# Top-k attention and a GELU block on one core: the search for the 32nd largest score split into sorted pairs, with the pairs' smaller halves made on GpSimd

## The chip, the cores and the metric

The kernel runs on one core of one Trainium2 chip. The metric is the device time of one execution in microseconds (us). Below, PE is the TensorE, DVE the VectorE, ACT the ScalarE, POOL the GpSimd and SP the SyncE, whose queue issues nearly all DMAs. All data is float32 in SBUF with 128 partitions; "128x576" means 128 partitions with 576 elements each.

## What is computed

For 8 batches of 8 heads with 576 tokens of 64 values each, the 32 largest scores of every row are kept, the rest is pushed to minus infinity, and the softmax of the row multiplies v. The result, put side by side by heads as 4608 tokens of 512 values, goes through two matrix products with an exact GELU between them.

```
scores = scale * np.matmul(q, k.transpose(0, 1, 3, 2))          # 576 x 576 per head
kth = np.partition(scores, -top_k, axis=-1)[..., -top_k:-top_k + 1]   # top_k = 32
scores = np.where(scores >= kth, scores, -1000000000.0)
scores = scores - np.max(scores, axis=-1, keepdims=True)
attn = np.exp(scores); attn = attn / (np.sum(attn, axis=-1, keepdims=True) + 1e-09)
attn_out = np.matmul(attn, v)
h = x @ w_in                                                     # 4608 x 512 by 512 x 2048
out = (0.5 * h * (1.0 + erf(h * inv_sqrt2))) @ w_out             # 2048 x 512
```

## The kernel before, in words

The attention works in 144 items. One item is 128 score rows of each of two heads, so two rows of 576 scores per partition (tile `s`, 128x1152, in five buffers). The main loop (L659) runs one step n per item and holds several items at once: in step n it forms the scores of item n+2 on PE and copies them to SBUF on ACT (L301, L302), searches item n on DVE (`top_k`, L329), does the softmax of item n-1 on ACT (L383 and L384), and transposes item n-2 on PE (L415, L433). Every second step multiplies a finished pair of items by v (L470) and copies the product to `xT` (L475). The rest of PE's time in a step goes to pieces of the two matrix products (L522 and L558), eight pieces a step as soon as enough tokens are in `xT`, which is from step 10 on. In the steps before that, `keep_busy` (L633) fills PE with multiplications whose result is thrown away. After the last item PE alone finishes the pieces that are left. The order on every engine is the order in which the code issues the instructions.

`top_k` finds the 32nd largest of 576 scores for both rows of an item: four rounds of MAX8 (the eight largest, L344), and after each of the first three a replacement of the eight found by a very small number (L347, which the profile shows as a short MATCH_VALUE_LOAD and a MATCH_REPLACE8). The hook in the last round is `inverse` (L370), DVE's reciprocal of the softmax sum of the item before; it waits for `add_small` (L376) on POOL, and that waits for the softmax on ACT.

POOL's order in a step is: the first addition of a weight block (`weights_add`, L198), `add_small` of item n-1 (L376), the second addition (`weights_end`, L210; it comes directly behind the first in the late units), `threshold` of item n (L359 and L362, which wait for the search), and `normalise` of item n-1 (L396, two multiplications of 128x576 by the reciprocal). PE's transposes of item n-1 in step n+1 wait for `normalise`.

The weights are brought in 16 units, loaded by SP from L160 as words shifted by two bytes and put together by ACT (L175, L177, L179) and POOL. Ten units are made in steps 1 to 10 (START is 10), six more in steps 13 to 18. In the six late units POOL also does ACT's third operation (L195), and `normalise` is done by DVE in five of those steps. Four of the units are staged in a tile of its own (`words`), the others in a part of `w_out_sb` that isn't used yet.

Of the kernel before, what the change touches and what calls it, by code (L numbers as in the profile page):

```python
# [8 lines left out]
TOPK = 32  # L9
LOWEST = -3.4028234e38  # L10
# [4 lines left out]
def kernel(  # L15
# [19 lines left out]
    nc = tc.nc  # L35
    f32, i32, u32 = mybir.dt.float32, mybir.dt.int32, mybir.dt.uint32
    bf16, i16, u16 = mybir.dt.bfloat16, mybir.dt.int16, mybir.dt.uint16
    AF = mybir.ActivationFunctionType
    ALU = mybir.AluOpType

    B, H, S, D = q.shape
    P = 128
# [12 lines left out]
    RING = 2 * S  # L55
# [4 lines left out]
    const = ctx.enter_context(tc.tile_pool(name="const", bufs=1))  # L60
    work = ctx.enter_context(tc.tile_pool(name="work", bufs=2))
# [6 lines left out]
    xT = const.tile([P, KO, RING], f32, name="xT")  # L68
# [39 lines left out]
    WS = 512  # L108
# [5 lines left out]
    def weights_of(u):  # L114

        if u < NWI:
            c, r = u // 2 * WS, u % 2 * 2
            return w_in, r, c, w_in_sb[:, r : r + 2, c : c + WS]
        r = 2 * (u - NWI)
        return w_out, r, 0, w_out_sb[:, r : r + 2, :]  # L120
# [5 lines left out]
    words = {}  # L126
# [11 lines left out]
    def load_weights(n, queue=None):  # L138

        queue = queue or nc.sync  # L140
        u = unit_in(n)
        if u is None:
            return
        src, r, c, dst = weights_of(u)
        if src.dtype == f32:
            for x in range(2):
                queue.dma_start(
                    out=dst[:, x], in_=src[(r + x) * P : (r + x + 1) * P, c : c + WS]
                )
            return  # L150


        half, i = src.bitcast(u16), ORDER.index(u)
        if i not in (2, 12, 14, 15):
            at = FT // 2 + 4 * (i % 2)
            t = w_out_sb[:, at : at + 4, :].rearrange("p (a b) n -> p a (b n)", a=2)
        else:
            t = stage.tile([P, 2, 2 * WS], f32, tag="words", name="words")
        for a in range(2):
            queue.dma_start(  # L160
                out=t[:, a].bitcast(u16)[:, 0 : 4 * WS - 1],
                in_=half[(r + a) * P : (r + a + 1) * P, 4 * c + 1 : 4 * (c + WS)],
            )
        words[u] = t

    def parts(u):

        t, dst = words[u], weights_of(u)[3].bitcast(i32)
        return t[:, :, 0::2], t.bitcast(mybir.dt.int16)[:, :, 2::4], t[:, :, 1::2].bitcast(i32), dst

    def weights_size(u):
        if u not in words:
# [8 lines left out]
    def on_pool(u):  # L181

        return u in words and SLOT_OF[u] > START

    def waits(u):

        return u == ORDER[-1]
# [3 lines left out]
    def weights_add(u):  # L191
        if u in words:
            w, _, below, d = parts(u)
            if on_pool(u):
                nc.gpsimd.tensor_scalar(  # L195
                    w.bitcast(i32), w.bitcast(u32), 2.0**-13, None, op0=ALU.mult
                )
            nc.gpsimd.tensor_tensor(d, d, below, op=ALU.add)  # L198
            if not ends_late(u):
                weights_end(u)  # L200
        made.add(u)

    def ends_late(u):

        return u in words and SLOT_OF[u] <= START

    def weights_end(u):
        if u in words:
            w, _, _, d = parts(u)
            nc.gpsimd.tensor_tensor(d, d, w.bitcast(i32), op=ALU.add)  # L210
# [3 lines left out]
    for b in range(B):  # L214
# [4 lines left out]
        last = [(b * NP + p, NM) for p in range(0, NP, 2)]  # L219
# [8 lines left out]
    N = len(items)  # L228
# [30 lines left out]
    S_of, stat_of = {}, {}  # L259

    def row(i, e):
        return S_of[i][:, e * S : (e + 1) * S]
# [14 lines left out]
    def scores(i):  # L277
# [25 lines left out]
        else:  # L303
# [22 lines left out]
                func=AF.Copy, scale=scale,  # L326
            )

    def top_k(i, hooks):  # L329


        stat_of[i] = st = {
            "top": work.tile([P, 2, TOPK], f32, tag="top", name="top"),
            "neg": work.tile([P, 2, 2], f32, tag="neg", name="neg"),
            "bias": work.tile([P, 2], f32, tag="bias", name="bias"),
            "den": work.tile([P, 2], f32, tag="den", name="den"),
            "rden": work.tile([P, 2], f32, tag="rden", name="rden"),
        }
        cur = [row(i, e) for e in range(2)]
        rest = work.tile([P, 2, S], f32, tag="rest", bufs=1, name="rest")  # L340
        n_op = 0
        for r in range(TOPK // 8):
            for e in range(2):
                nc.vector.max(st["top"][:, e, 8 * r : 8 * r + 8], cur[e])  # L344
            if r < TOPK // 8 - 1:
                for e in range(2):
                    nc.vector.match_replace(  # L347
                        rest[:, e], st["top"][:, e, 8 * r : 8 * r + 8], cur[e], LOWEST
                    )
                cur = [rest[:, e] for e in range(2)]  # L350
            if r in hooks:
                hooks.pop(r)()

    def threshold(i):

        if i < 0 or i >= N:
            return
        st = stat_of[i]
        nc.gpsimd.tensor_scalar(  # L359
            st["neg"], st["top"][:, :, 0 :: TOPK - 1], -1.0, None, op0=ALU.mult  # L360
        )
        nc.gpsimd.tensor_tensor(  # L362
            st["bias"], st["neg"][:, :, 0], st["neg"][:, :, 1], op=ALU.subtract
        )
# [24 lines left out]
    def normalise(i, on_dve):  # L389

        if i < 0 or i >= N:
            return
        st = stat_of[i]
        for e in range(2):
            s = row(i, e)
            (nc.vector if e >= 2 - on_dve else nc.gpsimd).tensor_scalar(  # L396
                s, s, st["rden"][:, e : e + 1], None, op0=ALU.mult
            )

    pt_now = [None]  # L400
# [43 lines left out]
    def copy_x():  # L444
        while copies:
            copies.pop()()
# [149 lines left out]
    def run_gelus():  # L596
        while waiting:
            gelus(waiting.pop(0))
# [20 lines left out]
    ready, left = [0], [0]  # L619

    eager = [False]
    staging = ExitStack()
    stage = staging.enter_context(tc.tile_pool(name="stage", bufs=1))

    load("k", 1)
    load("q", 1)
    for n in range(1, 3):
        load_weights(n)
# [25 lines left out]
    for pair in range(2, n_pairs):  # L654
        b, p = divmod(pair, NP)
# [3 lines left out]
    for n in range(ahead):  # L659

        left[0] = 4 if n in (START, START + 1) else 8
        eager[0] = n > N
        if not waits(unit_in(n)):
            weights_add(unit_in(n))
        scores(n + 2)
        product = attend(n - 3)
        late = n > START
        if n <= START:

            softmax(n - 1, 0)  # L670
        copy_x()
        if waits(unit_in(n)):
            weights_size(unit_in(n))
            weights_add(unit_in(n))
        mlp(1)
        tr = transposes(n - 2)
        if product and n > START and done[0] < len(pieces) and pieces[done[0]][0] > ready[0]:

            for piece in tr[:1]:
                piece()  # L680
            tr, ready[0] = tr[1:], n_tok[0]
        if n > START:
            softmax(n - 1, 0)
        mlp(1)
        if not late:
            softmax(n - 1, 1)
        mlp(1)
        if n < START:

            keep_busy((4 if product or n == 0 else 14) * (1 if n < 5 else 2), ident)  # L690
        prep = prep_in.pop(n, [])
        if n == START + 1:

            for piece in prep:
                piece()
            prep = []
        if len(prep) > 1 and len(tr) == 3:
            tr, prep = tr[:1] + prep[:1] + tr[1:], prep[1:]
        for piece in tr[:-1]:
            piece()  # L700
            if n < START and product and piece is tr[0]:
                keep_busy(5 if n < 5 else 10, ident)
            ready[0] = n_tok[0]
            mlp(1)
        ready[0] = n_tok[0]
        if late:
            softmax(n - 1, 1)
        add_small(n - 1)
        if ends_late(unit_in(n)):
            weights_end(unit_in(n))  # L710
        for piece in tr[-1:] + prep:
            piece()
            mlp(1)
        if n == 1:
            keep_busy(8, ident)

        run_gelus()
        mlp(left[0])
        run_gelus()
        if n < N:  # L720
            top_k(n, {3: lambda: inverse(n - 1)})
        else:
            inverse(n - 1)
        threshold(n)
        u = unit_in(n + 1)

        normalise(n - 1, 2 if on_pool(u) else 0)

        if not waits(unit_in(n + 1)):
            weights_size(unit_in(n + 1))  # L730
        for m in (n + 1, n + 2):

            if m > 2 and waits(unit_in(m)) == (m == n + 1):
                load_weights(m)
        if n <= NP:
            load("v", n)

    ready[0], left[0] = NT, len(pieces)
    while done[0] < len(pieces):
        mlp(1)  # L740
        run_gelus()
    staging.close()


# [30 lines left out]
```

## Time and profile before

| what | us |
|---|---|
| three timed runs, median | 1637.5 |
| lowest and highest of them | 1636.53 and 1637.75 |
| span of the profiled execution | 1634.7 |
| median of the timed runs less that span | 2.8 |
| PE busy in the span | 1611.5 |
| DVE busy | 1414.9 |
| ACT busy | 1185.3 |
| POOL busy | 665.3 |
| start of the reciprocal of the last item | 1557.3 |

The page gives no other time for the profiled execution than its span. "Busy" counts instructions at work; a busy PE is modelled and need not be PE at its peak. In the timelines each row has the start, the length, the engine, the line and the operation, with the number of merged instructions behind an x; the idle time in front of it and what ended that stand in brackets. Where two instructions follow each other without idle time, the distance of their starts is what one costs its engine; the length shown is some tens of ns more, since the next one begins before the last result is written. In the tables by windows each engine has its busy time in that stretch.

### The profile page before, as it was taken

To read this page: it belongs to the slowest core of one execution; us is meant where nothing else is said; L and a number is where in the kernel's file an instruction comes from. 1 tells how busy PE (TensorE), PEld (TensorE's weight loads), DVE (VectorE), ACT (ScalarE), POOL (GpSimd) and SP (SyncE) were. 2 spreads that over 40 slices of the span, in tenths; PEclk is the share of its full clock that TensorE was granted. 3 is DMA by queue.
4 is the path that set the end of the run, shared out by engine and by line. 5 is a ranking of instruction groups with operands and counts; after the bars stand their busy time and mean duration, and the time that the engine had idled before them with its cause. 6 is when DMAs were issued, how large, how long until landed. Compare 5 with 4: busy or idle time off the path is not lost.

```text
span 1634.7 us, 25758 instructions
## 1 busy us (share of the span) xinstructions
PE 1611.5 (99%) x9184; PEld 1105.8 (68%) x9184; DVE 1414.9 (87%) x3046; ACT 1185.3 (73%) x2132; POOL 665.3 (41%) x760
## 2 busy tenths in 40 slices
PE   7999999999999999999999999999999999999999
PEld 5776676766666666666666667676666666666665
DVE  8999999988898899998899899998889889999800
ACT  6989877777777777777777777777777777777720
POOL 4986833333333333333333333333333333333300
PEclk9999999999999999999999999999999999999999
DMA  6523210011101120001110111001110101000000
GB/s 165 157 76 117 81 43 1 14 40 33 36 1 28 30 58 1 14 19 33 29 28 15 28 30 43 1 14 36 37 36 1 28 16 36 1 14 4 4 14 13
DMA packets 126768, 56.19 MB, mean 34 GB/s; under 512 B 117776, under 2 KB 118064, under 8 KB 126640
## 3 DMA queue, kind: packets, MB, share of 16 engines
q1 hardware_dynamic: 125376, 54.12, 12.3%
q8 instruction: 73, 1.20, 0.3%
q10 hardware_dynamic: 1200, 0.39, 0.1%
q14 instruction: 55, 0.45, 0.1%
q0 software_dynamic: 64, 0.03, 0.0%
HBM read 45.08 MB, written 9.44 MB: 33 GB/s over the span
## 4 chain that ended last, share of the span: by engine, by line
PE 91%; DVE 5%; ACT 2%; POOL 1%; issue 0%; SPq 0%; DMA 0%; DVEq 0%; POOLq 0%; ACTq 0%
PE h_ps L522 30%; PE y_ps L558 30%; PE o L470 8%; PE s_ps L291 7%; PE tp L433 7%; DVE top L344 3%; DVE rest L347 2%; PE tp_qk L246 2%; PE t_ps L287 2%; PE o L481 1%; PE tp_t L415 1%; PE s_ps L318 1%; POOL s L396 1%; ACT s L384 0%; ACT s L383 0%
## 5 line engine op out<-in xcount | busy, mean ns | idle before, releaser
L344 DVE MAX8 top<-rest 128x8 f32<-128x576 f32 x864 | 610.0, 748 | 0.0
L522 PE MATMUL h_ps<-xT,w_in_sb 128*128 128x256 f32 (+1 forms) x2560 | 553.1, 361 | 0.0
L558 PE MATMUL y_ps<-w_out_sb,g 128*128 128x512 f32 x1152 | 548.9, 599 | 0.0
L396 POOL TENSOR_SCALAR s<-s,rden 128x576 f32<-128x576 f32 x278 | 476.5, 1723 | 0.6 <-DVE rden L370 0.4
L522 PEld LDWEIGHTS h_ps<-xT,w_in_sb 128*128 128x128 f32 x2560 | 428.4, 191 | 61.8 <-issue 16.4
L347 DVE MATCH_REPLACE8 rest<-top,rest 128x576 f32<-128x576 f32 x576 | 423.7, 744 | 0.0
L376 POOL TENSOR_SCALAR den<-den 128x2 f32<-128x2 f32 x144 | 32.0, 222 | 826.5 <-ACT s L384 826.0
L558 PEld LDWEIGHTS y_ps<-w_out_sb,g 128*128 128x128 f32 x1152 | 195.1, 190 | 168.2 <-issue 167.3
L301 ACT ACTIVATE s<-s_ps 128x1024 f32<-128x1024 f32 x127 | 130.6, 1028 | 164.9 <-PE s_ps L291 143.4
L384 ACT ACTIVATE s<-s,bias 128x576 f32<-128x576 f32 x288 | 223.4, 776 | 13.2 <-ACT s L383 0.7
L383 ACT ACTIVATE s<-s,neg 128x576 f32<-128x576 f32 x288 | 224.2, 778 | 0.3 <-POOL neg L359 0.2
L440 ACT COPY pt<-tp 128x512 f32<-128x512 f32 x256 | 146.8, 575 | 99.7 <-PE tp L433 99.6
L347 DVE MATCH_REPLACE8 rest<-top,s 128x576 f32<-128x576 f32 x288 | 211.9, 744 | 0.0
L433 PEld LDWEIGHTS tp<-ident,s 128*128 128x128 f32 x1152 | 142.5, 141 | 89.7 <-issue 58.9
L344 DVE MAX8 top<-s 128x8 f32<-128x576 f32 x288 | 201.9, 743 | 1.4 <-ACT s L297 1.4
L433 PE MATMUL tp<-ident,s 128*128 128x128 f32 x1152 | 172.7, 273 | 4.6 <-ACT pt L416 4.3
L470 PE MATMUL o<-pt,raw_v 128*64 128x256 f32 x1280 | 152.7, 385 | 0.5 <-ACT pt L440 0.5
L291 PE MATMUL s_ps<-qk 64*128 64x256 f32 x1024 | 146.1, 404 | 0.8 <-ACT s L299 0.8
L370 DVE RECIPROCAL rden<-den 128x2 f32<-128x2 f32 x144 | 23.2, 161 | 134.7 <-POOL den L376 134.4
L470 PEld LDWEIGHTS o<-pt,raw_v 128*64 128x64 f32 x1280 | 86.4, 137 | 64.4 <-issue 21.4
L533 ACT ACTIVATE g<-h_ps 128x512 f32<-128x512 f32 x144 | 78.6, 595 | 37.8 <-PE h_ps L522 37.1
L291 PEld LDWEIGHTS s_ps<-qk 64*128 64x128 f32 x1024 | 88.6, 187 | 22.2 <-ACT s L299 1.0
(77 smaller groups left out, 1155.7 us busy)
## 6 DMA issues: line engine op xcount, KB each, us to landing
raw_q<-in_q_dram SPq DMA_DIRECT2D x64, 128.0 KB, 2.4
raw_v<-in_v_dram SPq DMA_DIRECT2D x64, 128.0 KB, 2.5
raw_k<-in_k_dram SPq DMA_DIRECT2D x62, 128.0 KB, 2.5
out_dram<-y SPq DMA_DIRECT2D x31, 256.0 KB, 2.2
w_out_sb<-in_moe_w_in_dram SPq DMA_DIRECT2D x14, 511.8 KB, 5.1
w_out_sb<-in_moe_w_out_dram SPq DMA_DIRECT2D x10, 511.8 KB, 4.2
words<-in_moe_w_out_dram SPq DMA_DIRECT2D x6, 511.8 KB, 4.2
out_dram<-y SPq DMA_DIRECT2D x9, 128.0 KB, 2.3
```

Of the source, the lines that this page charges most:

```text
L291: nc.tensor.matmul(s_ps[:, e, c * 256 : (c + 1) * 256], lhsT=lhsT[rows, :], rhs=qk[rows, KT + c * 256 : KT + (c + 1) * 256], start=True, s ...
L301: nc.scalar.activation(spread(s, S + TL, SM), s_ps, func=AF.Copy, scale=scale)
L344: nc.vector.max(st["top"][:, e, 8 * r : 8 * r + 8], cur[e])
L347: nc.vector.match_replace(rest[:, e], st["top"][:, e, 8 * r : 8 * r + 8], cur[e], LOWEST)
L383: nc.scalar.activation(s, s, func=AF.Prelu, bias=st["neg"][:, e, 1:2], scale=1.0, alpha=STEEP)
L384: nc.scalar.activation(s, s, func=AF.Exp, bias=st["bias"][:, e : e + 1], scale=1.0, accum_out=st["den"][:, e : e + 1],)
L396: (nc.vector if e >= 2 - on_dve else nc.gpsimd).tensor_scalar(s, s, st["rden"][:, e : e + 1], None, op0=ALU.mult)
L433: nc.tensor.transpose(tp[:, j * P : (j + 1) * P], s[:, first + j * P : first + (j + 1) * P], ident)
L440: nc.scalar.copy(out=dst, in_=tp.rearrange("p (j n) -> p j n", j=NM))
L470: nc.tensor.matmul(o[e * D : (e + 1) * D, 0:n], lhsT=vt[:, j, e, :], rhs=pt[:, e * NM + j if j < NM else 2 * NM, :], start=(j == 0), stop= ...
L522: nc.tensor.matmul(h_tile(u)[:, i, :], lhsT=w_in_sb[:, ko, f * P : (f + 1) * P], rhs=xT[:, ko, c0 : c0 + n], start=(ko == 0), stop=(ko == ...
L558: nc.tensor.matmul(y_of[sub], lhsT=g_of[u][:, i, sub * P : (sub + 1) * P], rhs=w_out_sb[:, f, :], start=(f == 0), stop=(f == FT - 1),)
```

## The change

For every item the 576 scores of a row are split into 288 pairs, score j with score j + 288. A new function `fold` makes two tiles: the larger of each pair on DVE (two inputs of 128x576 in SBUF), and the smaller on POOL as a + b - larger, in integer arithmetic on the bits. `fold(n+1)` stands at the head of step n. `top_k` runs four rounds on the 288 larger scores and two rounds on the 288 smaller ones, replacing in place. The 32nd largest of all is then the largest of 17 minima, each of one entry of the falling list of the larger scores and one of the rising list of the smaller: a minimum of 128x34 and a reduction to 128x2 on DVE, behind the hook.

```
+    def fold(i):
+        if i >= N:
+            return
+        two = S_of[i].rearrange("p (e h n) -> p h e n", e=2, h=2)
+        high_of, low_of = HL_of[i] = [
+            work.tile([P, 2, S // 2], f32, tag=t, name=t) for t in ("high_of", "low_of")
+        ]
+        a, b, hi, lo = (t.bitcast(i32) for t in (two[:, 0], two[:, 1], high_of, low_of))
+        nc.gpsimd.tensor_tensor(lo, a, b, op=ALU.add)
+        nc.vector.tensor_tensor(high_of, two[:, 0], two[:, 1], op=ALU.max)
+        nc.gpsimd.tensor_tensor(lo, lo, hi, op=ALU.subtract)
...
+        def round_of(x, dst, last):
+            for e in range(2):
+                nc.vector.max(dst[:, e], x[:, e])
+            if not last:
+                for e in range(2):
+                    nc.vector.match_replace(x[:, e], dst[:, e], x[:, e], LOWEST)
+
         for r in range(TOPK // 8):
...
+            round_of(high_of, top[:, :, 8 * r : 8 * r + 8], r == TOPK // 8 - 1)
+            if r >= TOPK // 16:
+                x = r - TOPK // 16
+                round_of(low_of, low_top[:, :, 8 * x + 1 : 8 * x + 9], r == TOPK // 8 - 1)
             if r in hooks:
                 hooks.pop(r)()
...
+        nc.vector.tensor_tensor(both, rising, low_top, op=ALU.min)
+        nc.vector.tensor_reduce(
+            top[:, :, TOPK - 1 : TOPK], both, axis=mybir.AxisListType.X, op=ALU.max
+        )
...
+        if n == 0:
+            fold(0)
+        fold(n + 1)
         if not waits(unit_in(n)):
             weights_add(unit_in(n))
```

Three further edits go with it. The tile `words` is gone: the four units that used it are staged in the last 512 columns of `xT`, in four rows of half the length, so that each takes four DMAs instead of two. The multiplication of `normalise` (L396) and the late units' multiplication on POOL (L195) get a second operation, a multiplication by 1.0.

```
-            t = stage.tile([P, 2, 2 * WS], f32, tag="words", name="words")
+            t = xT[:, :, RING - WS :]
...
-                    w.bitcast(i32), w.bitcast(u32), 2.0**-13, None, op0=ALU.mult
+                    w.bitcast(i32), w.bitcast(u32), 2.0**-13, 1.0, op0=ALU.mult, op1=ALU.mult
...
-                s, s, st["rden"][:, e : e + 1], None, op0=ALU.mult
+                s, s, st["rden"][:, e : e + 1], 1.0, op0=ALU.mult, op1=ALU.mult
```

PE's instructions, the number of `keep_busy` multiplications among them, are the same as before.

More of the change, by code (lines that the diff above doesn't have):

```diff
@@ L157, in load_weights @@
         else:
-            t = stage.tile([P, 2, 2 * WS], f32, tag="words", name="words")
-        for a in range(2):
+            t = xT[:, :, RING - WS :]
+        n = 4 * WS // (t.shape[1] // 2)
+        for a in range(t.shape[1]):
+            row, at = divmod(a * n, 4 * WS)
+            end = min(at + n, 4 * WS - 1)
             queue.dma_start(
-                out=t[:, a].bitcast(u16)[:, 0 : 4 * WS - 1],
-                in_=half[(r + a) * P : (r + a + 1) * P, 4 * c + 1 : 4 * (c + WS)],
+                out=t[:, a].bitcast(u16)[:, 0 : end - at],
+                in_=half[(r + row) * P : (r + row + 1) * P, 4 * c + 1 + at : 4 * c + 1 + end],
             )
@@ L168, in parts @@
         t, dst = words[u], weights_of(u)[3].bitcast(i32)
-        return t[:, :, 0::2], t.bitcast(mybir.dt.int16)[:, :, 2::4], t[:, :, 1::2].bitcast(i32), dst
+        if t.shape[1] == 4:
+            t = t.rearrange("p (a b) n -> p a b n", a=2)
+            dst = dst.rearrange("p a (b n) -> p a b n", b=2)
+        return t[..., 0::2], t.bitcast(mybir.dt.int16)[..., 2::4], t[..., 1::2].bitcast(i32), dst
     def weights_size(u):
@@ L327, in scores @@
             )
+    HL_of = {}
+    HALF = TOPK // 2
+    low_tops = [const.tile([P, 2, HALF + 1], f32, name=f"low_top{x}") for x in range(2)]
+    for t in low_tops:
+        nc.vector.memset(t[:, :, 0:1], -LOWEST)
+    def fold(i):
[9 more added lines that the diff above has]
+        nc.gpsimd.tensor_tensor(lo, lo, hi, op=ALU.subtract)
     def top_k(i, hooks):
@@ L338, in top_k @@
         }
-        cur = [row(i, e) for e in range(2)]
-        rest = work.tile([P, 2, S], f32, tag="rest", bufs=1, name="rest")
-        n_op = 0
-        for r in range(TOPK // 8):
[L343 to L350, printed above, removed]
+        top, low_top, (high_of, low_of) = st["top"], low_tops[i % 2], HL_of.pop(i)
+        def round_of(x, dst, last):
[4 more added lines that the diff above has]
+                    nc.vector.match_replace(x[:, e], dst[:, e], x[:, e], LOWEST)
+        for r in range(TOPK // 8):
+            round_of(high_of, top[:, :, 8 * r : 8 * r + 8], r == TOPK // 8 - 1)
+            if r >= TOPK // 16:
+                x = r - TOPK // 16
+                round_of(low_of, low_top[:, :, 8 * x + 1 : 8 * x + 9], r == TOPK // 8 - 1)
             if r in hooks:
                 hooks.pop(r)()
+        both = work.tile([P, 2, HALF + 1], f32, tag="both", bufs=1, name="both")
+        falling = top[:, :, HALF - 1 :]
+        rising = bass.AP(
+            tensor=falling.tensor, offset=falling.offset + HALF,
+            ap=[list(falling.ap[0]), list(falling.ap[1]), [-1, HALF + 1]],
+        )
+        nc.vector.tensor_tensor(both, rising, low_top, op=ALU.min)
+        nc.vector.tensor_reduce(
+            top[:, :, TOPK - 1 : TOPK], both, axis=mybir.AxisListType.X, op=ALU.max
+        )
     def threshold(i):
@@ L621 @@
     eager = [False]
-    staging = ExitStack()
-    stage = staging.enter_context(tc.tile_pool(name="stage", bufs=1))
     load("k", 1)
@@ L741 @@
         run_gelus()
-    staging.close()
 _INS = ["q", "k", "v", "moe_w_in", "moe_w_out"]
```

## The prediction

> **What bounds the kernel now.** I read the engines' shares first, then the table by windows, then the timelines of POOL and DVE in the early steps.
>
> ```profile
> PE 1611.5 (99%) x9184; PEld 1105.8 (68%) x9184; DVE 1414.9 (87%) x3046; ACT 1185.3 (73%) x2132; POOL 665.3 (41%) x760
> ```
>
> DVE, whose work the change cuts, is at 87%, PE at 99%. A share is a mean over stages, so the windows decide (length, then busy PE, PEld, DVE, ACT, POOL):
>
> ```profile
> 58.68:68.40 9.72, 9.68 (x81) 8.53 (x81) 9.72 (x24) 9.37 (x16) 9.27 (x8) 1.00 0.45 140
> 68.40:78.10 9.70, 9.49 (x79) 7.55 (x76) 9.70 (x24) 9.35 (x16) 8.88 (x8) 1.00 0.32 110
> 300.00:600.00 300.00, 300.00 (x1643) 202.84 (x1640) 270.44 (x582) 221.14 (x405) 111.56 (x137) 1.00 0.12 28
> ```
>
> There are two stages. From about 204 us to the end of the items PE is busy every microsecond (300.00 of 300.00), with instructions that the change leaves alone. Nothing that DVE or POOL saves there can move the end. POOL is idle there for nearly two thirds of the time, and no matmul waits for anything after 204 us, so the new work is covered too. Up to step 10 (about 107 us) DVE is the one that is never idle, 9.70 us a step, but PE (9.5 to 9.7, mostly filling), ACT (9.4) and POOL (8.9 to 9.3) are close behind it. The change can move the time only there, and one for one: the first tokens decide when PE's fixed work begins.
>
> One early step of POOL, and the rows of one search on DVE:
>
> ```profile
> 59.15 0.24 POOL L359 TENSOR_SCALAR neg<-top 128x4 f32<-128x4 f32 x1
> 59.47 0.19 POOL L362 TENSOR_TENSOR bias<-neg 128x2 f32<-128x2 f32 x1
> 59.65 3.43 POOL L396 TENSOR_SCALAR s<-s,rden 128x576 f32<-128x576 f32 x2
> 63.04 2.41 POOL L198 TENSOR_TENSOR w_out_sb<-w_out_sb 128x1024 int32<-128x1024 int32 x1
> 65.75 0.22 POOL L376 TENSOR_SCALAR den<-den 128x2 f32<-128x2 f32 x1 [0.29 <-ACT s L384]
> 66.05 2.40 POOL L210 TENSOR_TENSOR w_out_sb<-w_out_sb 128x1024 int32<-128x1024 int32 x1
> 68.51 0.23 POOL L359 TENSOR_SCALAR neg<-top 128x4 f32<-128x4 f32 x1
> ```
>
> ```profile
> 19.87 1.40 DVE L344 MAX8 top<-s 128x8 f32<-128x576 f32 x2
> 21.19 0.07 DVE L347 MATCH_VALUE_LOAD rest<-top,s 128x8 f32 x1
> 21.25 0.74 DVE L347 MATCH_REPLACE8 rest<-top,s 128x576 f32<-128x576 f32 x1
> 21.91 0.08 DVE L347 MATCH_VALUE_LOAD rest<-top,s 128x8 f32 x1
> ```
>
> By distances of starts POOL's step is neg 0.31, bias 0.17, the two normalisations 3.42, first addition 2.45, den 0.30, second addition 2.38: 9.03 of 9.70. It has 0.67 us to spare.
>
> **DVE's sum.** MAX8 and MATCH_REPLACE8 cost 0.66 us each over 576 elements (19.87 to 21.19 is two), MATCH_VALUE_LOAD 0.065, the reciprocal of 128x2 0.07. Before: 14 x 0.66 + 6 x 0.065 + 0.07 = 9.70, which is the step. Between 0.07 for 2 elements and 0.66 for 576 the line gives 0.36 for 288. After: 12 MAX8 and 8 replacements, 20 x 0.36 = 7.20; 8 loads 0.52; the fold's maximum of 576 elements 0.65; the reciprocal 0.07; minimum and reduction, tiny but each waiting for the result in front of it, 0.45 together (0.07 apiece at the least, 0.3 apiece at the most by POOL's small row neg). Sum 8.9, a gain of 0.8. Each replacement now follows the MAX8 that it reads with only 0.36 between; MAX8's result lags its slot by 0.748 - 0.66 = 0.09, so I take nothing; 0.09 on all 20 would be 1.8, DVE 10.7.
>
> **POOL's sum.** *Fold.* The integer addition costs 2.38 for 1024 elements and 0.17 for 2 (bias), so 1.41 for 576; two of them, 2.82. *Normalise with two operations.* No row shows it. At the top it costs what the one-operation row does, 1.71 each, or more. At the bottom, POOL's memsets, 204 ns for 128 and 305 for 256 elements, give 0.10 + 0.79 ns an element: 0.56. The one-operation form needs 2.97 ns an element, more than the addition with two inputs (2.16), so what limits it isn't data but how it is executed, and another form may be quicker; the mask's row (0.29 us for 128x128, one input, one output), with the same 0.10 at the start, gives 0.95. I take 0.75, midway between memset and mask, the rows that do one pass: 1.5 for both instead of 3.42. *The port.* Where DVE runs an operation that uses two ports, POOL is held:
>
> ```profile
> 158.30 0.23 POOL L359 TENSOR_SCALAR neg<-top 128x4 f32<-128x4 f32 x1
> 158.53 0.95 DVE L396 TENSOR_SCALAR s<-s,rden 128x576 f32<-128x576 f32 x2
> ...
> 158.61 0.48 POOL L362 TENSOR_TENSOR bias<-neg 128x2 f32<-128x2 f32 x1
> ```
>
> bias takes 0.48 instead of 0.19 and ends as DVE's first multiplication does (158.53 + 0.52). Whether the fold's maximum, with its two SBUF inputs, does the same no row shows: between 0 and its 0.65 us a step (more, if POOL goes first; rival 3). I take 0.65, since the only row with the two engines together shows a hold to the end.
>
> The Trainium skill, "SBUF — State Buffer", section "Who interferes with whom", states that a DVE instruction with two SBUF inputs does contend with a GpSimd instruction that reads SBUF, and that the first to start keeps the pair for its whole length; it speaks against this change. By it the term is 0.65; without it, 0.
>
> New POOL step: 9.03 - 3.42 + 1.5 + 2.82 + 0.65 = 10.6 us. POOL becomes the bound, 0.9 above the old step; DVE (8.9, its maximum held until the second addition ends), ACT (9.4) and PE (9.5) wait for it.
>
> The skill's "GPSIMD Engine Reference", section "Engine selection", calls one-input work roughly line-rate; its clock of 1.2 GHz would make 576 elements 0.48 us (an estimate) and the step 10.1. This trace's one-operation row, at 1.71, disagrees.
>
> **The sum.** *Head.* The first search started at 10.21. Now fold(1) stands before it and needs item 1's copies, which end at 13.09: the maximum ends at 13.8, the search at 22.0 and the first neg starts at 22.2 instead of 20.05. POOL then has neg, bias, fold, both additions and den, 8.4, ending at 31.1; with the maximum in between the second neg starts at 31.75 instead of 30.60. *Steps 2 to 10.* 9 x 10.6 = 95.4: neg of step 10 at 127.2 instead of 117.12. Normalise follows, 0.48 + 1.5: done at 129.2. PE's first tile of step 11 started at 121.73 and needs it: 7.5 late. *Steps 11 to 18.* The six late units add 2.82 of fold on POOL and lose about 1.8 at L195 (3.1 now, by the two rows above 0.9 to 1.6); DVE normalises in five, 0.52 each as in its row (doubled, 1.0 a step), and the transposes there start 3.2 us or more after it (137.45 to 140.62), so I add 0.5. *DMA.* Four staged units cost eight more issues of 0.4 to 0.6 on SP; behind the first stand loads of v that are first used in step 4, behind the others SP idles (156.9 to 164.6): nothing, 1 us if not covered. *Afterwards* PE is full: nothing. Sum +8.0: a profiled span of 1642.7. The median of the runs lies 2.8 above the old span: **1645.5 us**.
>
> With 0.56 for a normalisation the same sum gives +4, with 0.95 +12: the forecast's own range is 1641 to 1650.
>
> **Rivals.** (1) *POOL keeps up, no slowdown.* The maximum doesn't hold POOL, at the fold of each early step: POOL's step is 9.96 and PE's tile 1 us late. With 0.56 a normalisation it is 9.6, the transposes find their input earlier, and the 2.6 us in which PE waited between 107 and 129 us can go; then ACT at 9.4 and PE at 9.5 set the step. It decides from a POOL step of 9.8 downwards. 1635 to 1639. At the very best, 9 x 0.2 + 2.6 less 1.1 at the head, it gains 3.3. For it: no row has such a hold for two inputs. Against: the hold at 158.61. (2) *The second operation brings nothing*, the edit does not do what it may be for: 1.71 stays. The step is 12.5 (11.9 without hold), normalise of step 9 ends 21 to 27 us late, and the late steps, now 13 to 14 on POOL against 11.5, add 8 to 10: 1666 to 1674. For it: the nearest row, the same instruction. Against: its 2.97 ns beside 2.16 for two inputs. (3) *POOL goes first at the port.* The maximum waits for neg, bias, normalise and the first fold half, 3.4 us; the search starts after it: 3.4 + 0.65 + 7.7 + 0.7 = 12.4 a step, +24: 1661. Against: the maximum asks while the second addition runs, before neg.
>
> **How the numbers follow.** Forecast 50%, rival 1 22%, rival 2 19%, rival 3 9%. What a measurement can tell from no change is 0.2%, 3.3 us. Faster needs rival 1 beyond its best sum: 6%. Within: the rest of rival 1, and the lowest edge of the forecast: 20%. Slower: 74%. The range takes in rival 1, the forecast, rival 3 and the part of rival 2 without hold: 1635 to 1668; outside are the dearest form of rival 2 (some 12%) and a few per cent below.
>
> **What would show it.** Right: in the early windows POOL is never idle, its step 10.2 to 11.0 and DVE's 8.9 of work; the fold's maximum waits for, or lengthens, a POOL row; normalise on POOL 0.6 to 0.95; after 220 us PE full as before. Wrong: a normalisation at 1.7 or over, an addition of 576 elements far from 1.4, MAX8 above 0.45, POOL idle in the early steps, or PE idle in the long stage.

## The result, and the profile after

| | median, us | lowest to highest, us | against before |
|---|---|---|---|
| before (4 runs on this chip) | 1637.55 | 1636.53 to 1637.75 | |
| after (4 runs) | 1653.38 | 1652.39 to 1654.42 | 1.0099, interval 1.0087 to 1.0111 |

The change costs 15.8 us, about 1%. The profiled execution of after took 1652.39 us, with a span of 1650.6, 15.9 above the old span. The forecast was 1645.5. Slower is right, and the time lies inside the whole range of 1635 to 1668, but outside the 1641 to 1650 that the forecast gave for itself: the loss is twice the 8.0 that was worked out. In the experiments below, one execution of e5 (3838 us) and one of e11 (2765 us) stand far outside the others of their kernel and are left out of the ratios.

The engines' shares, then the windows of two early steps and of the long stage (length, then busy PE, PEld, DVE, ACT, POOL, the granted clock, DMA share and GB/s):

```profile
PE 1619.0 (98%) x9184; PEld 1112.7 (67%) x9184; DVE 1301.5 (79%) x4632; ACT 1187.4 (72%) x2132; POOL 848.3 (51%) x1048
```

```profile
43.57:54.37 10.80, 6.78 (x32) 4.53 (x32) 10.77 (x34) 9.10 (x16) 10.10 (x9) 0.68 0.61 166
54.37:65.17 10.80, 10.70 (x91) 8.96 (x88) 10.77 (x34) 9.93 (x17) 10.10 (x9) 1.00 0.48 142
300.00:600.00 300.00, 300.00 (x1621) 202.51 (x1621) 244.05 (x881) 222.24 (x406) 146.60 (x195) 1.00 0.11 27
```

DVE did lose 113 us of work over the whole span, and in the long stage that is worth nothing: PE is still busy for 300.00 of 300.00. The early step has grown from 9.70 to 10.80. DVE looks full in it (10.77), but the next two timelines show that part of that is held time (an operation is held when it lasts longer than it does alone, until an operation of the other engine ends). POOL's step, neg to neg, with the addition in front of it:

```profile
40.95 2.42 POOL L216 TENSOR_TENSOR w_in_sb<-w_in_sb,w_out_sb 128x1024 int32<-128x1024 int32 x1
43.75 0.66 POOL L396 TENSOR_SCALAR neg<-top 128x4 f32<-128x4 f32 x1 [0.37 <-DVE top L387]
44.49 0.20 POOL L399 TENSOR_TENSOR bias<-neg 128x2 f32<-128x2 f32 x1
44.66 1.48 POOL L433 TENSOR_SCALAR s<-s,rden 128x576 f32<-128x576 f32 x2
46.10 1.43 POOL L350 TENSOR_TENSOR low_of<-s 128x576 int32<-128x576 int32 x1
47.60 1.41 POOL L352 TENSOR_TENSOR low_of<-low_of,high_of 128x576 int32<-128x576 int32 x1
48.98 2.39 POOL L204 TENSOR_TENSOR w_in_sb<-w_in_sb,xT 128x1024 int32<-128x1024 int32 x1
51.46 0.22 POOL L413 TENSOR_SCALAR den<-den 128x2 f32<-128x2 f32 x1
51.76 2.41 POOL L216 TENSOR_TENSOR w_in_sb<-w_in_sb,xT 128x1024 int32<-128x1024 int32 x1
54.54 0.66 POOL L396 TENSOR_SCALAR neg<-top 128x4 f32<-128x4 f32 x1 [0.37 <-DVE top L387]
```

POOL has no slack except 0.37 us in front of neg, and neg takes 0.66 instead of 0.24. DVE around the same neg (POOL's addition ran from 40.95 to 43.37):

```profile
41.17 0.14 DVE L407 RECIPROCAL rden<-den 128x2 f32<-128x2 f32 x1
41.28 2.15 DVE L386 TENSOR_TENSOR both<-top,low_top 128x34 f32<-128x34 f32 x1
43.46 0.19 DVE L387 TENSOR_REDUCE top<-both 128x2 f32<-128x34 f32 x1
43.57 0.75 DVE L351 TENSOR_TENSOR high_of<-s 128x576 f32<-128x576 f32 x1
```

A minimum over 34 elements takes 2.15 us: it ends at 43.43, just behind POOL's addition. The reduction after it takes 0.19. Then the fold's maximum runs from 43.57 to 44.32, and POOL's neg, started at 43.75, ends just behind it. Each engine is held once a step, and each time by the operation of the other that started first.

At step 18 stands a wait that before did not have. PE in before, PE in after, and ACT in after a little ahead of it:

```profile
195.44 0.30 PE L420 MATMUL tp_t<-ident,s 128*64 128x128 f32 x1
196.45 0.30 PE L420 MATMUL tp_t<-ident,s 128*64 128x128 f32 x1 [0.71 <-POOL s L396]
200.06 4.48 PE L522 MATMUL h_ps<-xT,w_in_sb 128*128 128x256 f32 x20
```

```profile
206.75 0.73 PE L457 MATMUL tp_t<-ident,s 128*64 128x128 f32 x2
207.32 0.60 PE L559 MATMUL h_ps<-xT,w_in_sb 128*128 128x256 f32 x2
211.79 2.90 PE L559 MATMUL h_ps<-xT,w_in_sb 128*128 128x256 f32 x6 [3.88 <-ACT xT L183]
216.34 4.48 PE L559 MATMUL h_ps<-xT,w_in_sb 128*128 128x256 f32 x20
```

```profile
209.16 1.23 ACT L181 ACTIVATE w_out_sb<-xT,low 128x1024 int32<-128x1024 int16 x1 [1.86 <-DMA xT<-in_moe_w_out_dram]
210.42 1.23 ACT L183 ACTIVATE xT<-xT,high 128x1024 int32<-128x1024 int16 x1
```

L183 works in place on the staged words of the last weight unit, which now lie in the last 512 columns of `xT`. PE wants other columns of the same tile and waits for it. The six matmuls behind the wait take 2.90 us, where four of the same kind take 1.03 a little later; between 211.79 and 214.60 the granted clock is 0.50. PE is 11.3 late in front of this place (206.75 against 195.44) and 16.3 behind it (216.34 against 200.06).

### The profile page after: what moved, and what is told of

Same layout as the page of the kernel before. It is cut to its first block, busy times and chain, and to the rows that moved or that the text cites. A ratio compares the mean times of both kernels' runs of the same rounds, so it can differ in the third digit from the quotient of the medians.

```text
span 1650.6 us, 27661 instructions
## 1 busy us (share of the span) xinstructions
PE 1619.0 (98%) x9184; PEld 1112.7 (67%) x9184; DVE 1301.5 (79%) x4632; ACT 1187.4 (72%) x2132; POOL 848.3 (51%) x1048
## 4 chain that ended last, share of the span: by engine, by line
PE 91%; DVE 6%; ACT 1%; POOL 0%; DMA 0%; issue 0%; SPq 0%; ACTq 0%; DVEq 0%
PE h_ps L559 31%; PE y_ps L595 30%; PE o L507 8%; PE s_ps L297 7%; PE tp L470 7%; PE tp_qk L252 2%; DVE top L368 2%; DVE high_of L371 2%; PE t_ps L293 2%; PE o L518 1%; DVE both L386 1%; PE s_ps L324 1%; PE tp_t L452 1%; DVE low_top L368 1%; DVE low_of L371 1%; DVE high_of L351 0%
## 5 line engine op out<-in xcount | busy, mean ns | idle before, releaser
L368 DVE MAX8 top<-high_of 128x8 f32<-128x288 f32 x1152 | 467.5, 447 | 0.0
L371 DVE MATCH_REPLACE8 high_of<-top,high_of 128x288 f32<-128x288 f32 x864 | 376.1, 443 | 0.0
L368 DVE MAX8 low_top<-low_of 128x8 f32<-128x288 f32 x576 | 232.7, 446 | 0.0
L350 POOL TENSOR_TENSOR low_of<-s 128x576 int32<-128x576 int32 x144 | 208.1, 1445 | 7.8 <-ACT s L305 7.8
L352 POOL TENSOR_TENSOR low_of<-low_of,high_of 128x576 int32<-128x576 int32 x144 | 203.4, 1413 | 11.3
L433 POOL TENSOR_SCALAR s<-s,rden 128x576 f32<-128x576 f32 x278 | 205.5, 751 | 0.4 <-DVE rden L407 0.4
L396 POOL TENSOR_SCALAR neg<-top 128x4 f32<-128x4 f32 x144 | 93.2, 647 | 92.0 <-DVE top L387 92.0
```

The lines of the kernel that those rows point to most:

```text
L350: nc.gpsimd.tensor_tensor(lo, a, b, op=ALU.add)
L352: nc.gpsimd.tensor_tensor(lo, lo, hi, op=ALU.subtract)
L368: nc.vector.max(dst[:, e], x[:, e])
L371: nc.vector.match_replace(x[:, e], dst[:, e], x[:, e], LOWEST)
```

## Experiments

Theory: what the change costs is POOL's fold in the early steps, two holds between DVE and POOL in each of them, and the shared tile at step 18. Rivals: the search on DVE or the second operation costs more than it seems; the head, where the first neg came 3.6 us later, makes the loss; or a slower late stage does.

Four groups of kernels each shared a chip and its runs of the kernel before (medians 1637.45 for e1 to e4, 1637.16 for e5 to e8, 1637.38 for e9 and e10, 1637.46 for e11). "Loss" is the median less that of before on the same chip.

| kernel | median, us | ratio to before, interval | loss, us | early step, us |
|---|---|---|---|---|
| after | 1653.38 | 1.0087 to 1.0111 | 15.8 | 10.80 |
| e3_one_op | 1685.30 | 1.0275 to 1.0305 | 47.9 | 12.75 |
| e2_one_input_max | 1649.50 | 1.0056 to 1.0086 | 12.1 | 10.38 |
| e9_one_input_min | 1650.51 | 1.0066 to 1.0093 | 13.1 | 10.49 |
| e1_split_xt | 1648.87 | 1.0052 to 1.0086 | 11.4 | 10.81 |
| e10_no_hold | 1640.11 | 1.0009 to 1.0027 | 2.7 | 9.99 |
| e4_smaller_on_dve | 1639.00 | 1.0003 to 1.0021 | 1.6 | 9.53 |
| e8_min_and_split | 1636.70 | 0.9989 to 1.0007 | -0.5 | 9.53 |
| e6_head | 1653.07 | 1.0084 to 1.0112 | 15.9 | 10.80 |
| e7_all | 1636.80 | 0.9990 to 1.0007 | -0.4 | 9.53 |
| e5_before_two_op | 1636.22 | 0.9983 to 1.0001 | -0.9 | 9.6 |
| e11_shared | 1637.17 | 0.9991 to 1.0009 | -0.3 | 9.30 |

The early step is the distance of neg to neg between 60 and 80 us.

**The second operation taken away (e3).** Is it worth what the prediction gave it?

```
-                w.bitcast(i32), w.bitcast(u32), 2.0**-13, 1.0, op0=ALU.mult, op1=ALU.mult
+                w.bitcast(i32), w.bitcast(u32), 2.0**-13, None, op0=ALU.mult
...
-                s, s, st["rden"][:, e : e + 1], 1.0, op0=ALU.mult, op1=ALU.mult
+                s, s, st["rden"][:, e : e + 1], None, op0=ALU.mult
```

> The changed kernel without the second operation in the two POOL multiplications. Theory: POOL sets the early step, so every microsecond more on it counts: a normalisation at 1.71 instead of 0.74 makes the step 12.75 and nine steps 17.5 us, the normalisation behind the last another 2, and the late units 2 us a step for some of six: 1672 to 1683. Rival: the early step is set by DVE waiting in turn for POOL and the longer normalisation hides there: under 5 us more.

Two normalisations on POOL, in the timeline of e3 (after has 1.48 for them):

```profile
72.11 3.43 POOL L433 TENSOR_SCALAR s<-s,rden 128x576 f32<-128x576 f32 x2
```

The step grows by 1.95, as the theory has it, and the loss by 32 us, more than expected: in the late units, where L201 costs 2.95 instead of 1.14, a step takes 13.1 instead of 11.3 too, and PE's waits for POOL's normalisation sum to 33 us. The second operation does what it is for. It is a gain inside the change, not a cost.

**The two holds (e2, e9).** Neither wait was taken away; the operation was replaced by one that reads the same numbers through a single input, a reduction over pairs. e2 does so for the fold's maximum, e9 for the small minimum, whose two lists then lie in one tile, the second in reverse.

```
-        nc.vector.tensor_tensor(high_of, two[:, 0], two[:, 1], op=ALU.max)
+        nc.vector.tensor_reduce(
+            high_of, S_of[i].rearrange("p (e h n) -> p e n h", e=2, h=2),
+            axis=mybir.AxisListType.X, op=ALU.max,
+        )
```

> The changed kernel with the fold's maximum as a reduction over the pair axis (one SBUF input of 1152 elements instead of two of 576; the same result). Theory: the hold of POOL's neg (0.66 instead of 0.23 us) comes from the second SBUF input; neg goes back to 0.23, the early step from 10.80 to 10.3 to 10.4 (the small minimum still waits for the second addition), and the time falls by 3 to 4.5 us, to about 1649.5, although DVE works 0.5 us more a step. Rival: neg is long for another reason, or DVE's longer step is late: neg stays, within 1 us of 1653.4.

```
-        nc.vector.tensor_tensor(both, rising, low_top, op=ALU.min)
+        pairs = tops[i % 2][:, :, :, HALF - 1 :].rearrange("p e h n -> p e n h")
+        nc.vector.tensor_reduce(both, pairs, axis=mybir.AxisListType.X, op=ALU.min)
```

> The kernel after with the small minimum at the end of the search read as one input: both sorted lists lie in one tile, the smaller ones' in reverse, and a reduction by minimum over pairs takes the place of the operation with two inputs. Theory: the 2.15 us of that operation over 34 elements are a hold by POOL's second addition; read through one input it takes 0.2 us or less, ends before that addition does, and the 0.37 us in which POOL waits for neg go. Early step 10.43 instead of 10.80, nine steps: 3.3 us less, 1649.5 to 1651. Rival: the operation waits for something else (the lists' last write, the queue) and stays at 2 us: early step 10.8, 1653 to 1654.

POOL in e2, then DVE and POOL in e9:

```profile
61.01 2.42 POOL L216 TENSOR_TENSOR w_in_sb<-w_in_sb,w_out_sb 128x1024 int32<-128x1024 int32 x1
63.81 0.23 POOL L399 TENSOR_SCALAR neg<-top 128x4 f32<-128x4 f32 x1 [0.37 <-DVE top L390]
```

```profile
61.85 0.23 DVE L389 TENSOR_REDUCE both<-top 128x34 f32<-128x68 f32 x1
62.11 0.19 DVE L390 TENSOR_REDUCE top<-both 128x2 f32<-128x34 f32 x1
62.22 2.35 DVE L351 TENSOR_TENSOR high_of<-s 128x576 f32<-128x576 f32 x1
```

```profile
61.53 2.42 POOL L216 TENSOR_TENSOR w_in_sb<-w_in_sb,w_out_sb 128x1024 int32<-128x1024 int32 x1
63.92 0.73 POOL L399 TENSOR_SCALAR neg<-top 128x4 f32<-128x4 f32 x1
```

In e2 neg is back at 0.23 and the 0.37 in front of it stays: 0.42 a step, 3.8 us. In e9 the minimum takes 0.23 in the midst of POOL's second addition (61.53 to 63.95), and the 0.37 is gone: 0.31 a step, 2.7 us. But now the fold's maximum, two inputs again, starts during that addition and takes 2.35 instead of 0.75: it ends at 64.57, 0.62 behind the addition, and neg, started at 63.92, takes 0.73. In these rows the hold goes with the operation that has two inputs, and taking one away hands a part of it on.

The Trainium skill, "SBUF — State Buffer", section "Who interferes with whom", says that a DVE instruction with two SBUF inputs contends with a GpSimd instruction that reads SBUF, that `tensor_reduce` never does on trn2, and that order of issue decides who is blocked. These runs agree: 2.15 against 0.23 us for the small operation, 0.66 against 0.23 for neg, and the engine that started later is the one that is held in every row shown.

**The shared tile (e1).** The tile `xT` becomes two, `xT_a` with 640 columns and `xT_b` with the 512 that also serve as staging; nothing else changes.

```
-    xT = const.tile([P, KO, RING], f32, name="xT")
+    xT_a = const.tile([P, KO, 640], f32, name="xT_a")
+    xT_b = const.tile([P, KO, 512], f32, name="xT_b")
```

> The changed kernel with xT as two tiles (the first 640 columns, and the last 512, in which the late weight words are staged), so that a first-product matmul on the first columns shares no tile with the staged words. Theory: the 3.9 us for which PE stood before a first-product matmul in step 18, and the slower matmuls just behind it, come from the shared tile; they go, and the time falls by 4 to 5.5 us, to about 1648.5. Rival: the weight units would be late for PE anyway, and another wait takes the place: within 1 us of 1653.4.

PE at the same place in e1:

```profile
206.05 0.30 PE L461 MATMUL tp_t<-ident,s 128*64 128x128 f32 x1
206.55 0.30 PE L461 MATMUL tp_t<-ident,s 128*64 128x128 f32 x1 [0.20 <-POOL s L437]
206.69 1.89 PE L563 MATMUL h_ps<-xT_a,w_in_sb 128*128 128x256 f32 x8
208.41 0.60 PE L474 MATMUL tp<-ident,s 128*128 128x128 f32 x4
208.85 1.03 PE L563 MATMUL h_ps<-xT_a,w_in_sb 128*128 128x256 f32 x4
211.58 0.66 PE L474 MATMUL tp<-ident,s 128*128 128x128 f32 x4 [1.70 <-ACT ptt L466]
```

PE's products run straight on: the wait came from sharing a tile, not from shared columns. The loss falls by 4.4, from 15.8 to 11.4. The staged words still come late for ACT (L185 waits 1.99 for its DMA), the copy `ptt` is queued behind that, and PE waits 1.70 for it instead. So the edit takes away 3.6 of the 5.0 that arise here: PE is 10.6 late in front of this place (206.05) and 12.0 behind it (212.07). The other 0.7 us by which e1 is ahead of after stood before step 18 already, half of it at the second neg (32.59 against 32.93); what made them is not shown.

**All three together (e10).** e1, e2 and e9 in one kernel, so that no operation of DVE in an early step reads two SBUF inputs. The diff is the three above.

> The kernel after with three edits: the small minimum and the fold's maximum both read as one input (as in e9 and e2), and the layer's input as two tiles (as in e1). No operation of VectorE with two SBUF inputs is left in an early step. Theory: the three losses are separate and add up, 4.5 for the tile, 3.9 for the maximum, 3.3 for the minimum: early step 10.0, 1640 to 1643, and what is left above the kernel before, 3 to 6 us, is POOL's fold itself. Rival: with the holds gone another engine sets the step, or VectorE, whose maximum now takes 1.37 us, does: early step 10.4, 1645 or more.

One step of POOL in e10:

```profile
62.39 0.23 POOL L406 TENSOR_SCALAR neg<-top 128x4 f32<-128x4 f32 x1
62.71 0.20 POOL L409 TENSOR_TENSOR bias<-neg 128x2 f32<-128x2 f32 x1
62.88 1.48 POOL L443 TENSOR_SCALAR s<-s,rden 128x576 f32<-128x576 f32 x2
64.32 1.41 POOL L354 TENSOR_TENSOR low_of<-s 128x576 int32<-128x576 int32 x1
65.81 1.42 POOL L359 TENSOR_TENSOR low_of<-low_of,high_of 128x576 int32<-128x576 int32 x1
67.19 2.41 POOL L208 TENSOR_TENSOR w_out_sb<-w_out_sb 128x1024 int32<-128x1024 int32 x1
69.69 0.22 POOL L423 TENSOR_SCALAR den<-den 128x2 f32<-128x2 f32 x1
69.99 2.43 POOL L220 TENSOR_TENSOR w_out_sb<-w_out_sb 128x1024 int32<-128x1024 int32 x1
72.38 0.23 POOL L406 TENSOR_SCALAR neg<-top 128x4 f32<-128x4 f32 x1
```

POOL never idles and is never held: 9.99 us, the bare sum of its rows. The three single gains were 4.4, 3.8 and 2.7, in sum 10.9; together they give 13.1, which is the same within the intervals (some 2 us each). Most of what is left, 2.7 us, is POOL's fold and the head: the second neg comes 1.85 later than before's, each of nine steps adds 0.38 (9.99 less 9.61), and 2.6 come back, 2.0 of them by the shorter normalisation, so that PE's first tile of step 11 starts at 124.38, where before had it at 121.73: 2.65 late. At step 18 PE waits 1.77 for `ptt`, which adds 1.1 (203.86 against 200.06 is 3.8 late); the profiled span is 3.4 longer than before's.

**The fold taken off POOL (e4, then e8 with the split tile).**

```
-        nc.gpsimd.tensor_tensor(lo, a, b, op=ALU.add)
         nc.vector.tensor_tensor(high_of, two[:, 0], two[:, 1], op=ALU.max)
-        nc.gpsimd.tensor_tensor(lo, lo, hi, op=ALU.subtract)
+        nc.vector.tensor_tensor(low_of, two[:, 0], two[:, 1], op=ALU.min)
```

> The changed kernel with the smaller halves as a minimum on DVE (0.65 us) in place of POOL's two integer operations (2.86 us). Theory: POOL's fold is the cost; DVE's step becomes 9.55, POOL's 7.6 and the early step 9.6 to 9.8 instead of 10.80: 9 to 11 us less, about 1643. Rival: the two-input operations on DVE are the cost, and with two of 576 elements a step DVE waits for POOL oftener: an early step of 10.4 or more, 1649 or over.

> The kernel after with two edits together: the smaller ones by a minimum on VectorE (as in e4) and the layer's input as two tiles (as in e1). Theory: the early step stays at 9.53, and the wait of TensorE for the shared tile, 1.7 us in e4, goes: 1636.5 to 1638, the same as the kernel before. Rival: that wait is covered once POOL has time, and nothing is added to e4's gain: 1638.5 to 1639.5.

POOL in e8, at the turn of a step:

```profile
61.19 0.66 POOL L398 TENSOR_SCALAR neg<-top 128x4 f32<-128x4 f32 x1 [0.82 <-DVE top L389]
61.93 0.55 POOL L401 TENSOR_TENSOR bias<-neg 128x2 f32<-128x2 f32 x1
62.47 1.47 POOL L435 TENSOR_SCALAR s<-s,rden 128x576 f32<-128x576 f32 x2
```

The maximum holds neg and the minimum holds bias (0.55 instead of 0.20), so the holds are no shorter than in after. But POOL now idles 0.82 in front of neg, so they cost nothing. DVE sets the step: 8.86 of search and 0.67 for the minimum are 9.53. e4 gains 14.4 us, better than was expected of it, and with the split tile the last 1.6 us go too: 0.67 us of DVE do what 2.86 us of POOL did.

**The head (e6), and with e8 (e7).** The fold of item 1 stands behind the search of item 0.

```
-        fold(n + 1)
+        if n > 0:
+            fold(n + 1)
...
             top_k(n, {3: lambda: inverse(n - 1)})
+            if n == 0:
+                fold(1)
```

> The kernel after with one thing moved: the fold of item 1 stands behind the search of item 0 on VectorE instead of ahead of it. Theory: the 3.6 us by which the first neg was later than before come from this fold, whose maximum waits for item 1's scores; about 2 us of it come back at the first neg, but the fold's work is then late for the second, so that 1 to 2.5 us are left: 1651 to 1652.4. Rival: POOL's chain from the first step on absorbs it, nothing changes: 1653.0 to 1653.8.

> The kernel after with three edits: minimum on VectorE, the input as two tiles, the fold of item 1 behind the search of item 0. Theory: the early step of 9.53 instead of 9.65, over nine steps, gives 1 us against the kernel before, the head is within 1 us of it, the second operation shortens the late steps' normalisation: 1633.5 to 1636.5, a little under the kernel before. Rival: the head's gain is taken up by the next steps: the same as e8_min_and_split within 1 us.

POOL in e6:

```profile
23.14 1.79 POOL L352 TENSOR_TENSOR low_of<-low_of,high_of 128x576 int32<-128x576 int32 x1 [7.05 <-DVE high_of L351]
24.90 0.23 POOL L396 TENSOR_SCALAR neg<-top 128x4 f32<-128x4 f32 x1
```

The theory fell. The number is the rival's, for a third reason: POOL works in order, its second half of fold 1 now waits 7.05 us for DVE's maximum, and the first neg, ready earlier, is queued behind it at 24.90 (23.61 in after). In e7, where POOL has no part in the fold, the first neg does come at 20.30, but the second at 31.16, later than before's 30.60, and the time is that of e8.

**The second operation alone (e5, with e5b for a profile).** The kernel before with the two lines of e3's diff the other way round.

> The kernel before (search over 576 pairs, no fold) with one part of the change alone: the second operation in POOL's two multiplications. Theory: the saving of about 2 us a step on POOL is real but POOL had slack there, since the search on VectorE at 9.70 us a step stays as it is; only the waits of TensorE for POOL's normalisation between 107 and 129 us (2.6 us in all) can go. 1634 to 1636.5. Rival: ScalarE and the search hold everything and nothing at all is gained: 1637 to 1638. In the trace: POOL's step stays at 9.6 to 9.75, with about 2 us of idle time in it.

> The same kernel as e5 (the kernel before with the second operation), for a profile. Theory: POOL's early step stays at 9.6 to 9.75 with 1.9 us or more of idle time in it, TensorE's waits for POOL's normalisation between 107 and 129 us are gone, and the search of 9.70 on VectorE sets the step. Rival: POOL's step is shorter than VectorE's and something else moved.

POOL in e5b:

```profile
71.09 0.23 POOL L359 TENSOR_SCALAR neg<-top 128x4 f32<-128x4 f32 x1
71.41 0.19 POOL L362 TENSOR_TENSOR bias<-neg 128x2 f32<-128x2 f32 x1
71.58 1.47 POOL L396 TENSOR_SCALAR s<-s,rden 128x576 f32<-128x576 f32 x2
73.02 2.41 POOL L198 TENSOR_TENSOR w_out_sb<-w_out_sb 128x1024 int32<-128x1024 int32 x1
78.01 0.22 POOL L376 TENSOR_SCALAR den<-den 128x2 f32<-128x2 f32 x1 [2.57 <-ACT s L384]
```

POOL saves 1.96 us a step and spends 2.57 idle: the search holds the step at 9.6. PE's 2.7 us of waits for POOL's normalisation between 60 and 240 us are gone, a wait of 1.2 for ACT's copy of scores has taken a part of their place, and 0.9 us come out, with an interval that reaches 1.0001. Of the 2.6 us that the expectation counts between 107 and 129 us only 1.35 were waits for POOL; the others ended with copies of ACT. It is the only part of the change that points to a gain by itself, and it is too small to call. e5b's own time (1637.45, a single run) adds nothing to that: in that execution one step, from 49.53 to 61.47, took 11.94. PE's 20 multiplications by v took 4.30 there, where before had 2.79, at a granted clock of 0.71 between 50 and 61 us, and ACT waited 1.03 for them; that this makes the whole difference is not shown.

**The best form that the rows point to (e11).** e1 and e9, with the fold shared: the smaller scores of one head by POOL, those of the other by DVE's minimum.

```
+        a, b, hi, lo = (
+            t.bitcast(i32) for t in (two[:, 0, 0], two[:, 1, 0], high_of[:, 0], low_of[:, 0])
+        )
...
+        nc.vector.tensor_tensor(low_of[:, 1], two[:, 0, 1], two[:, 1, 1], op=ALU.min)
```

> The kernel after with the fold shared between the engines, to see whether any form of this search beats the kernel before: the smaller ones of one head by POOL's two additions, those of the other by a minimum on VectorE; the small minimum as one input (as in e9); the input as two tiles (as in e1). From the rows: VectorE loses half of e8's 0.67 of minimum, 9.53 becomes about 9.25 a step; POOL gets half of 2.86 on top of e8's 8.6, about 9.4 with a hold; so the step is about 9.4, against 9.65 before. Theory: nine steps give 2 us against the kernel before, less about 1 us for the head: 1635 to 1637, faster by no more than 0.15%. Rival: the minimum and the maximum hold POOL in turn, POOL's step goes over 9.7: 1638 to 1641.

The early step is the shortest of all, 9.30, and the time is that of before (ratio 1.0000, interval 0.9991 to 1.0009). PE's first tile of step 11 starts at 122.46, 0.7 later than before's: the second neg is 2.2 us later (32.78 against 30.60), and the nine steps from there give back only 1.45, since two of them, from 98 us on, take 9.7 and 9.9. By the rows of before a faster early step is worth a few us at most, since ACT (9.4) and PE (9.5) are nearly as long as DVE; no version that beats before was found.

## Why the prediction was right and wrong, step by step

**Right.** *What bounds the kernel*: PE full from 220 us on, DVE's 113 us of savings worth nothing, POOL the bound of the early steps. *DVE's sum*: the search runs at 0.36 for 288 elements, without the lag that it feared. *The fold*: 2.86 a step on POOL, forecast 2.82. *Normalise with two operations*: 1.44 for both by the distance of starts, forecast 1.5; that it hit the middle between memset and mask is partly luck, since no row of before showed the form. Rival 2 is out; its kernel is e3, which lost 47.9 us where the rival was priced at 28.5 to 36.5. From the Trainium skill's "GPSIMD Engine Reference", section "Engine selection", which calls one-input work roughly line-rate, the prediction had worked out an estimate of 0.48; this form's row took 0.75, 1.6 times that, and the one with a single operation (1.72) 3.6 times. *Late units*: forecast 0.5 later. PE's step 18 (L457) starts at 206.75 against 195.44, 11.3 late, as at step 11: nothing is lost in between. Nor does a later stage make the loss: PE is 16.3 late behind step 18, and the span is 15.9 longer.

**Wrong, first step: DMA and staging, "nothing, 1 us if not covered".** The step asked only what the extra DMA issues cost. It left out that ACT and POOL work in place on the staged words, and that they now do so in a tile which PE reads; nor had the sum a term for PE's clock behind a wait. PE waits 3.88 us, and its next six matmuls take 2.90 where about 1.5 would be their time (e4, after a wait of 1.67, has 1.53 for six). With 0.3 in their neighbours, less the 0.6 that PE lost in before at this place, 5.0 arise here, over half of the miss of 7.9. e1 takes 3.6 of them away; 1.4 stay as the wait for `ptt`. In e8, where the fold is off POOL too, none are left (200.59 against 200.06 behind this place, 196.26 against 195.44 in front of it).

**Wrong, second step: the head, 31.75 for the second neg.** It came at 32.93, 2.33 later than before instead of 1.15. The fold's maximum of item 1 was reckoned with 0.7 us and took 1.70 (13.61 to 15.31), because POOL's L352 was running from 13.29 to 14.70 when it started; item 1's copies ended at 13.58 instead of 13.09. The term also had an error of addition in its favour: 22.2 and 8.4 end at 30.6, not at 31.1, so its own rows give 31.25. The prediction had priced the hold of POOL by DVE; the hold of DVE by POOL it had left to rival 3, where POOL would come first.

**Wrong, third step: the port, 0.65 a step.** There are two holds, not one. neg behind the maximum costs 0.43, and the small minimum, priced at 0.07 to 0.3, is held until the second addition ends and costs POOL 0.37 of idle time: 0.80. With small differences in the other rows POOL's step was 10.80 instead of 10.6, nine times 0.2, 1.8 us. PE's tile of step 11 then comes 2.83 behind the last neg (130.17 to 133.00), where 2.0 were forecast, 0.8 more. The hold of that neg is 0.43 of it; the rest is PE's own, which waited 3.56 in front of step 10's first tile (121.87), ran at a granted clock of 0.58 from there to 125.87, and had no wait in front of the tile at 133.00.

Summed: 7.5 forecast for PE's tile in step 11, plus 1.2 at the head, 1.8 over nine steps and 0.8 at the end, is 11.3, which is what the trace has (133.00 against 121.73). With 5.0 for the staged words PE is 16.3 late behind step 18; the spans differ by 15.9.

*Rival 1*, POOL keeps up without a hold, had 9.96 for POOL's step, PE's tile 1 us late and 1635 to 1639. e10 is the kernel of that rival, with 9.99, 2.65 late and 1640.1. *Rival 3*, POOL first at the port, happened in mild form: it is DVE's small minimum that is held in each step, and the maximum at the head; the maximum in the steps came first. What was only argued: that the holds come about at a port. The runs show which operations hold and which do not, and who waits for whom, not by which wire. e2 and e9 also put another instruction (TENSOR_REDUCE) in place of TENSOR_TENSOR, and no run changes the number of inputs alone. Nor does any run take the loss at the head away: e6 and e7 only move it.

## What to carry to other kernels

Count an operation's cost on the engine that takes it over, in the stage that matters: here 0.8 us a step came off DVE, and 2.86 of fold and 0.8 of holds, less 1.98 of normalisation, went to POOL, which had 0.67 to spare. When two engines share work on small tiles, look at every row with two inputs, however short, and ask which row of the other engine it meets; a reduction over pairs reads the same data through one. Here work in place in one part of a tile made PE wait 3.88 us for other columns of it: give staged data a tile of its own.

## What the runs showed of the hardware that was not expected

- A multiplication on POOL with a second operation (times 1.0) takes 0.75 us for 128x576 instead of 1.72, and 1.14 instead of 2.95 for 128x1024 (after against e3).
- The length of an operation does not limit how long it is held: 34 elements took 2.15 us beside a running POOL addition, 0.20 or less where POOL was idle.
- Some of PE's waits cost more than their length. After 3.7 to 4.1 us of idling at step 18 (after, e2, e9) the next six matmuls took 2.90 and the granted clock between 200 and 220 us was 0.83 to 0.91; after 1.67 us (e4) they took 1.53, at a clock of 1.00. Elsewhere in after, a wait of 2.75 us was followed by a clock of 0.50 (78.61 to 80.00) and one of 3.56 by 0.58 (121.87 to 125.87); after waits of 1.50 (after, at 100.25), 1.70 (e1) and 1.77 (e10) it stayed at 1.00.
